# Immediates for the Ln, and features laid out in pairs of heads

## Chip, core and metric

The kernel runs on one core of a Trainium2 chip. Its time is the device time of one execution in microseconds, as a median over runs. The engines are named as in the profile: PE (TensorE, matmuls; PEld is its weight load), DVE (VectorE), ACT (ScalarE), POOL (GpSimd) and SP (SyncE, which issues most DMAs).

## The reference, cut to what matters

Two layers of linear attention with an exponential feature map, each followed by a gated MLP, over 2048 tokens of 512 elements, 32 heads of 16:

```python
def _A_ref(x, wqkv, w_phi, wo):
    ...
    pq = jnp.einsum("bhsd,hdf->bhsf", q, w_phi)
    pk = jnp.einsum("bhsd,hdf->bhsf", k, w_phi)
    phi_q = jnp.concatenate([_softmax(pq, axis=-1), _softmax(-pq, axis=-1)], axis=-1)
    phi_k = jnp.concatenate([_softmax(pk, axis=-1), _softmax(-pk, axis=-1)], axis=-1)
    kv = jnp.einsum("bhsf,bhsd->bhfd", phi_k, v)
    z  = jnp.einsum("bhsf->bhf", phi_k)
    num = jnp.einsum("bhqf,bhfd->bhqd", phi_q, kv)
    den = jnp.einsum("bhqf,bhf->bhq", phi_q, z)[..., None] + 1e-6
    o = num / den
    return (...o...) @ wo
...
x = x + _A_ref(_layernorm(x, axis=-1), A_wqkv, A_w_phi, A_wo)
x = x + _B_ref(_layernorm(x, axis=-1), B_W_gate, B_W_up, B_W_down)
x = x + _A_ref(_layernorm(x, axis=-1), A_wqkv, A_w_phi, A_wo)
x = x + _B_ref(_layernorm(x, axis=-1), B_W_gate, B_W_up, B_W_down)
```

A softmax over 16 features does not change when the last feature is subtracted from all, so the kernel folds that into the weights: 15 exponentials are computed, the 16th is 1, and the sum that scales them is 1 plus the sum of the 15.

## The kernel before, in words

The 2048 tokens are 16 tiles of 128 rows (partitions). The order of every instruction on every engine is written out in a list (ORDER), as are the buffers that each step takes (SLOTS) and, for steps that two engines can do, the engine (PLACE). Nothing is decided at run time: each engine works through its own list and waits on semaphores, and SP's DMAs are issued in the order of the list too.

For a tile of **keys** (class Keys): statistics of x on DVE (L510, L511), then the reciprocal standard deviation on ACT as exp(-0.5 ln(v + eps)) (L518 is the Ln with `bias=eps[:]`, L520 the Exp, rsA), the normalized tile xn on DVE or POOL (L534, L532), a transpose of it (PE L500 or SP L495), then the K matmul with folded weights (PE L596), the V matmul (PE L601) and its copy to SBUF (vext, L453 or L454). Two Exp of 480 elements on ACT (L568, one with scale 1 and one with -1) write the features into an `ek` tile; a reduction on DVE sums 64 groups of 15 (L606, sk); Ln with `bias=unit[:]` (L615, lnk) and Exp with scale -1 (L618, rk) on ACT make the 64 scales and put them into the same tile; a multiplication in two halves of 480 elements (L554, phi) on POOL or DVE scales the features; and the kvz matmuls (PE L629) add them up over all tiles.

An `ek` tile has 8 groups of 128 columns, a group for 4 heads. Before, a group is 60 positive features, 60 negative ones, and 8 scales at its end:

```python
e.tensor_tensor(out=v, in0=v, in1=ek.t[:, lo:lo + n, 2 * GF:P].unsqueeze(3).to_broadcast(
    [P, n, 2 * HG, DF]), op=Alu.mult)
```

so each scale is read 15 times at step 0, against 15 adjacent features.

For a tile of **queries**: the matmul (PE L656), the same two Exp, a reduction (L661, sq), Ln with the unit bias (L666) and Exp (L668) on half of the sums, the ratio on DVE (L672), one multiplication of 480 elements (L677, POOL or DVE), and a DMA transpose of the tile (SP L682, fq). Queries use tiles whose last constants were set to one at the start (ONES, on POOL).

When the keys of all tiles are done, R is built from their sums and a mask Mg on DVE (L641, L646); Mg is made at the start from the identity (L435, L437, L439). Then come, tile by tile, erq (PE L693), its division (L700 to L707), a transpose of o, the projection (PE L716), the residual sum (L720), and the MLP in blocks of 1 to 4 tiles (gate and up PE L793 and L769, down PE L833). The first layer's keys come first; the second layer's keys are worked in between the first layer's MLP blocks. The weights for queries are folded while the keys run: wq is loaded (SP, L866), transposed by DMA (SP L467) and multiplied (PE L481).

Of the kernel before, what the change touches and what calls it, by code (L numbers as in the profile page):

```python
# [8 lines left out]
P = 128  # L9
D = 512  # L10
H = 32
DH = 16
# [6 lines left out]
HB = 8  # L19
NG = 2 * NB  # L20
HG = HB // 2
# [3 lines left out]
DF = DH - 1  # L25
GF = HG * DF
FW = H * DF
EPS = 1e-5
DEN_EPS = 1e-6

Alu = mybir.AluOpType
AF = mybir.ActivationFunctionType
AX = mybir.AxisListType
BF16 = mybir.dt.bfloat16
F32 = mybir.dt.float32
# [89 lines left out]
DVE0 = (85, 170)  # L125
# [3 lines left out]
NOTHING = (0, 0)  # L129
# [151 lines left out]
def kernel(  # L281
    ctx: ExitStack, tc: tile.TileContext, A_x, A_wqkv, A_w_phi, A_wo, B_x, B_W_gate, B_W_up,
    B_W_down, out):
    nc = tc.nc
# [8 lines left out]
    def new(name, shape, dt=BF16):  # L293
        return sb.tile([P] + shape, dt, name=name)
# [14 lines left out]
    wf = new("wf", [NB, DH])  # L309
    wgu, wd = new("wgu", [2, NB, F]), new("wd", [NF, D])  # L310
    ident = new("ident", [P])
    Mf, Mg, Mh = new("Mf", [HB], F32), new("Mg", [HG], F32), new("Mh", [HG], F32)
    Wblk = new("Wblk", [NB, HB * DF])
    R = new("R", [NG, GE])
    xnTA = [new(f"xnTA{c}", [C, NB, P]) for c in range(C)]
    eps, unit = new("eps", [1], F32), new("unit", [1], F32)
    rowsum, ssq = new("rowsum", [2, T], F32), new("ssq", [2, T], F32)
    wasteA, wasteD = new("wasteA", [D]), new("wasteD", [D])
    st = {(l, s): (new(f"bst{s}{l}", [T, 6], F32), new(f"mv{s}{l}", [T, 2], F32),
# [25 lines left out]
    def op(eng, cost, due, emit, deps=(), takes=(), uses=(), name="", **kw):  # L345
        o = Op(eng, cost, due, emit, deps, takes, uses, name, **kw)
        ops.append(o)
        return o
# [52 lines left out]
    def first_constants():  # L401
        make_identity(nc, ident[:])
        for i in ONES:
            nc.gpsimd.memset(p_eq.tiles[i][:, :, 2 * GF + HG:P], 1.0)
    c_id = op("POOL", (900, 900), 0, first_constants, name="ident")
    def constants():
        nc.vector.memset(eps[:], EPS)
        nc.vector.memset(unit[:], 1.0)
    c_eps = op("DVE", DVE0, 0, constants, name="eps")
    ones = [op("DVE", DVE0, i, (lambda v: lambda: nc.vector.memset(v[:, :, GQ:GV], 1.0))(v), name="ones")  # L410
            for i, v in enumerate(p_v.tiles)]

    hr_zero = [op("DVE", dve(4 * (P - FR), 4), 9000, (lambda v: lambda: nc.vector.memset(v[:, :, FR:P], 0.0))(v),
                  name="hr0", port=True) for v in p_hr.tiles]
# [17 lines left out]
    c_blk = op("DVE", (640, 740), 20, lambda: blocks(nc.vector), [c_m, c_cen], name="Wblk", port=True,  # L432
               alt=("POOL", (1016, 1058), lambda: blocks(nc.gpsimd), 3))
    def state_masks():
        nc.vector.tensor_reduce(out=Mg[:], in_=ident[:, 0:2 * GF].rearrange("p (s h f) -> p h s f", s=2, f=DF),  # L435
                                axis=AX.XY, op=Alu.add)
        nc.vector.tensor_reduce(out=Mh[:], in_=ident[:, 2 * GF:P].rearrange("p (s h) -> p h s", s=2), axis=AX.X,  # L437
                                op=Alu.add)
        nc.vector.tensor_tensor(out=Mg[:], in0=Mg[:], in1=Mh[:], op=Alu.add)  # L439
    c_mg = op("DVE", (400, 490), 15000, state_masks, [c_m], name="Mg")  # L440
    wps = Buf(p_q)

    one = nc.const_aps.tensor(1.0, (P, 512), BF16)
# [69 lines left out]
    def norm_A(l, tiles, dues, afters, by_pe=False):  # L513

        _, mv, rs, ln = st[l, "A"]
        t0, n = tiles[0], len(tiles)
        seen = [stats(l, "A", t, due, after) for t, due, after in zip(tiles, dues, afters)]
        a = op("ACT", ACT1, dues[-1], lambda: nc.scalar.activation(  # L518
            out=ln[:, t0:t0 + n], in_=mv[:, t0:t0 + n, 1], func=AF.Ln, scale=1.0, bias=eps[:]), seen + [c_eps], name="ln")
        a = op("ACT", ACT0, dues[-1], lambda: nc.scalar.activation(  # L520
            out=rs[:, t0:t0 + n], in_=ln[:, t0:t0 + n], func=AF.Exp, scale=-0.5), [a], name="rstd")
        made, i = [], 0
        while i < n:
            k = 1 if by_pe or i + 1 == n else 2
            xn, scaled = Buf(p_xn), []
            for j in range(k):
                t = tiles[i + j]

                def on_pool(t=t, j=j, xn=xn):
                    nc.gpsimd.tensor_scalar(out=nm[:, t:t + 1], in0=mv[:, t, 0:1], scalar1=-1.0, scalar2=0.0,  # L530
                                            op0=Alu.mult, op1=Alu.add)
                    nc.gpsimd.tensor_scalar(out=xn.t[:, j], in0=x_of(t), scalar1=nm[:, t:t + 1],  # L532
                                            scalar2=rs[:, t:t + 1], op0=Alu.add, op1=Alu.mult)
                scaled.append(op("DVE", SCALE, dues[i + j], lambda t=t, j=j, xn=xn: nc.vector.tensor_scalar(  # L534
                    out=xn.t[:, j], in0=x_of(t), scalar1=mv[:, t, 0:1], scalar2=rs[:, t:t + 1],
                    op0=Alu.subtract, op1=Alu.mult), [a], [] if j else [xn], [xn] if j else [], name="xnA", port=2,
                    alt=("POOL", (930, 975), on_pool, 3) if l == 0 else None))
            c, r = tiles[i] // C, tiles[i] % C
            made += [turn(xn, lambda c=c, r=r, k=k: xnTA[c][:, r:r + k], k, dues[i], scaled, [], [], "xnTA",
                          by_pe)] * k  # L540
            i += k
        return made


    def features(ek, lo=0, n=NG):
        return ek.t[:, lo:lo + n, 0:2 * GF].rearrange("p g (j f) -> p g j f", f=DF)

    def halves(name, ek, engs, due, after, uses):
        parts = []
        n = NG // len(engs)  # L550

        def phi(e, lo):
            v = features(ek, lo, n)
            e.tensor_tensor(out=v, in0=v, in1=ek.t[:, lo:lo + n, 2 * GF:P].unsqueeze(3).to_broadcast(  # L554
                [P, n, 2 * HG, DF]), op=Alu.mult)
        for k, e in enumerate(engs):
            ways = {"DVE": ("DVE", dve(480), lambda k=k: phi(nc.vector, k * n), 1),
                    "POOL": ("POOL", (956, 998), lambda k=k: phi(nc.gpsimd, k * n), 3)}
            _, cost, f, _ = ways[e]
            parts.append(op(e, cost, due, f, after, [], uses, name=name,  # L560
                            port=ways[e][3], alt=ways["POOL" if e == "DVE" else "DVE"]))
        return parts

    def raised(ek, ps, s, side):
        assert side == "K" or ek.slot in ONES and ek.slot not in spoilt
        if side == "K":
            spoilt.add(ek.slot)
        nc.scalar.activation(out=ek.t[:, :, s * GF:(s + 1) * GF], in_=ps.t[:, 0:FW].rearrange(  # L568
            "p (g e) -> p g e", e=GF), func=AF.Exp, scale=1.0 - 2.0 * s)

    class Keys:
        def __init__(self, l, before):
# [8 lines left out]
        def begin(self, sk, row, t, due, due_v, due_z, xT, phi_eng, v_eng="ACT"):  # L581
# [13 lines left out]
            else:  # L595
# [8 lines left out]
            v = evac(v_eng, due_v, lambda: vx.t[:, :, 0:GQ], lambda: vp.t[:].rearrange("p (b e) -> p b e", e=GQ),  # L604
                     [v] + ones, [vx], [vp], "vext")
            a = op("DVE", SUM16, due, lambda: nc.vector.tensor_reduce(  # L606
                out=sk.t[:, row, :].rearrange("p (g j) -> p g j", g=NG), in_=features(ek), axis=AX.X, op=Alu.add),
                e, [] if row else [sk], [ek, sk] if row else [ek], name="sk")
            self.sk.append(a)
            self.ks.append(k)  # L610
# [2 lines left out]
        def finish(self, begun):  # L613
            (done, v, sk, ek, *rest), due = begun[0], begun[0][5]
            a = op("ACT", RLN[0], due, lambda: nc.scalar.activation(  # L615
                out=sk.t[:, 0, :], in_=sk.t[:, 0, :], func=AF.Ln, scale=1.0, bias=unit[:]), [done, c_eps], (), [sk],
                name="lnk")
            a = op("ACT", REXP[0], due, lambda: nc.scalar.activation(  # L618
                out=ek.t[:, :, 2 * GF:P], in_=sk.t[:, 0, :].rearrange("p (g j) -> p g j", g=NG), func=AF.Exp,
                scale=-1.0), [a], (), [sk, ek], name="rk")  # L620
            self.scale(a, v, ek, *rest)

# [30 lines left out]
    def query(l, t, due, xT, behind, key):  # L653
# [4 lines left out]
            for b in range(NB)], [xT] + q_fold, [qp, ek], name="Q", follow=key)  # L658
        e = [op("ACT", act(FW), due, lambda s=s: raised(ek, qp, s, "Q"), [q], (), [qp, ek], name="Eq")
             for s in range(2)]  # L660
        a = op("DVE", SUM16, due, lambda: nc.vector.tensor_reduce(  # L661
            out=sq.t[:].rearrange("p (g j) -> p g j", g=NG), in_=features(ek), axis=AX.X, op=Alu.add),
            e, [sq], [ek], name="sq", follow=behind)
        pos, neg = (lambda: sq.t[:].rearrange("p (g s h) -> p g s h", s=2, h=HG)[:, :, 0, :],
                    lambda: sq.t[:].rearrange("p (g s h) -> p g s h", s=2, h=HG)[:, :, 1, :])
        a = op("ACT", RLN[0], due, lambda: nc.scalar.activation(  # L666
            out=pos(), in_=pos(), func=AF.Ln, scale=1.0, bias=unit[:]), [a, c_eps], (), [sq], name="lnq")
        a = op("ACT", REXP[0], due, lambda: nc.scalar.activation(  # L668
            out=pos(), in_=pos(), func=AF.Exp, scale=-1.0), [a], (), [sq], name="rq")

        def ratio():
            nc.vector.scalar_tensor_tensor(out=ek.t[:, :, 2 * GF:2 * GF + HG], in0=neg(), scalar=1.0, in1=pos(), op0=Alu.add,  # L672
                                   op1=Alu.mult)

        def scale(e):
            v = ek.t[:, :, 0:GF].rearrange("p g (h f) -> p g h f", f=DF)
            e.tensor_tensor(out=v, in0=v, in1=ek.t[:, :, 2 * GF:2 * GF + HG].unsqueeze(3).to_broadcast(  # L677
                [P, NG, HG, DF]), op=Alu.mult)
        a = op("DVE", DVE0, due, ratio, [a], [], [ek, sq], name="rat", port=1, alt=("DVE", DVE0, ratio, 1))
        a = op("POOL", (956, 998), due, lambda: scale(nc.gpsimd), [a], [], [ek], name="phq", port=3,  # L680
               alt=("DVE", dve(480), lambda: scale(nc.vector), 1))
# [270 lines left out]
```

## Time and profile before

| | |
|---|---|
| median of 3 runs | 372.12 us (371.65 to 372.27) |
| profiled execution | 371.77 us |
| its span, first to last instruction | 370.0 us |
| PE busy | 361.4 us, 98% |
| DVE busy | 272.0 us, 74% |
| ACT busy | 203.4 us, 55% |
| POOL busy | 86.6 us, 23% |
| granted TensorE clock | 1.000 |

The span leaves out 1.77 us of the execution. Busy times are averages over stages that have different limits, so a row for one stretch of the span says more than the share of the whole. The ends of matmuls are modelled, so a busy PE need not be one at its peak. In a row of a group, the first two numbers behind the bar are its busy time in us and the mean duration of one in ns, and behind the second bar stands the idle time of the engine just before such instructions, with what ended it.

### The profile page before, as it was taken

The numbers are of one execution on the slowest core, as the hardware profiler recorded it, in microseconds if no ns is written. First come the engines' busy times: TensorE is split into PE (matmuls) and PEld (weight loads), VectorE is DVE, ScalarE is ACT, GpSimd is POOL, SyncE is SP. The second block draws the span as 40 slices with busy tenths as digits, with TensorE's granted clock in tenths as the row PEclk, the third lists the DMA queues.
The fourth block names the chain that finished last, engine by engine and source line by source line (L and its number), as shares of the span: only waits on it lengthen the run. The fifth ranks groups of instructions, "written<-read, shape, count | busy, mean of one in ns | idle before, by whom it ended". The sixth has DMA issues, their size and how long they took to land.

```text
span 370.0 us, 7444 instructions
## 1 busy us (share of the span) xinstructions
PE 361.4 (98%) x2803; PEld 217.0 (59%) x2845; DVE 272.0 (74%) x604; ACT 203.4 (55%) x549; POOL 86.6 (23%) x111
## 2 busy tenths in 40 slices
PE   8999999999999999999999999999999999999996
PEld 5454557776555454555666655686755454467484
DVE  6999999988798966848979498898976373233253
ACT  5999999662544860587274455874434226403130
POOL 4589754510030116004213173120000000000000
PEclk9999999999999999999999999999999999999999
DMA  8997776796653501113411210498752102010213
GB/s 239 195 225 161 235 123 128 128 151 126 96 101 58 99 16 30 37 22 64 85 36 31 57 32 0 69 134 121 137 99 45 28 0 44 0 44 0 81 54 98
DMA packets 93925, 31.73 MB, mean 86 GB/s; under 512 B 85345, under 2 KB 92865, under 8 KB 93889
## 3 DMA queue, kind: packets, MB, share of 16 engines
q1 hardware_dynamic: 93088, 30.98, 42.4%
q8 instruction: 22, 0.36, 0.4%
q10 hardware_dynamic: 800, 0.28, 0.3%
q14 instruction: 15, 0.11, 0.1%
HBM read 8.44 MB, written 2.10 MB: 28 GB/s over the span
## 4 chain that ended last, share of the span: by engine, by line
PE 84%; ACT 9%; DVE 2%; issue 1%; DMA 1%; POOL 1%; SPq 0%; DVEq 0%; ACTq 0%
PE b L793 38%; PE b L833 20%; PE b L716 7%; ACT ek L568 4%; PE b L601 4%; PE b L596 4%; PE b L656 4%; PE b L769 3%; PE q L693 2%; PE q L629 1%; ACT vext L453 1%; DMA X<-in_A_x_dram 1%; DVE sq L661 1%; ACT sk L615 1%; PE b L500 1%
## 5 line engine op out<-in xcount | busy, mean ns | idle before, releaser
L793 PE MATMUL b<-xnTB,wgu 128*128 128x128 bf16 (+2 forms) x1200 | 152.5, 279 | 0.1
L793 PEld LDWEIGHTS <-wgu 128*128 128x128 bf16 x1200 | 97.4, 98 | 47.2 <-issue 0.3
L797 ACT ACTIVATE gu<-b 128x512 bf16<-128x512 f32 (+1 forms) x83 | 47.6, 581 | 89.9 <-PE b L793 83.0
L833 PE MATMUL b<-wd,hT 128*128 128x512 bf16 (+3 forms) x340 | 83.2, 372 | 1.3
L568 ACT ACTIVATE ek<-b 128x480 bf16<-128x480 f32 x128 | 69.9, 597 | 16.1 <-PE b L596 8.6
L554 POOL TENSOR_TENSOR ek<-ek 128x480 bf16<-128x480 bf16 x48 | 49.5, 1055 | 79.2 <-ACT ek L618 74.6
L833 PEld LDWEIGHTS <-hT 128*128 128x128 bf16 (+1 forms) x363 | 34.3, 98 | 34.0 <-DVE hT L810 0.3
L810 DVE TENSOR_TENSOR hT<-gu,b 128x512 bf16<-128x512 bf16 (+1 forms) x44 | 28.6, 657 | 30.3 <-ACT gu L797 13.7
L677 POOL TENSOR_TENSOR ek<-ek 128x480 bf16<-128x480 bf16 x26 | 26.4, 1023 | 73.7 <-DVE ek L672 55.9
L661 DVE TENSOR_REDUCE sq<-ek 128x64 f32<-128x960 bf16 x32 | 36.4, 1144 | 4.1 <-ACT ek L568 4.1
L606 DVE TENSOR_REDUCE sk<-ek 128x64 f32<-128x960 bf16 x32 | 36.0, 1138 | 2.5 <-ACT ek L568 2.5
L801 DVE TENSOR_TENSOR hT<-gu 128x512 bf16<-128x512 bf16 (+1 forms) x39 | 17.2, 442 | 22.6 <-ACT gu L812 22.4
L840 DVE SCALAR_TENSOR_TENSOR X<-b,rsB,X 128x512 bf16<-128x512 f32 (+2 forms) x33 | 23.7, 729 | 12.9 <-PE b L833 12.7
L716 PE MATMUL b<-wo,oT 128*128 128x512 bf16 x117 | 30.8, 379 | 1.1 <-ACT oT L453 0.4
L601 PE MATMUL b<-wv,xnTA 128*128 128x512 bf16 x120 | 30.9, 379 | 0.6 <-ACT vext L453 0.2
L656 PE MATMUL b<-Wq,xnTA 128*128 128x480 bf16 x128 | 30.5, 365 | 0.1
L596 PE MATMUL b<-Wk,xnTA 128*128 128x480 bf16 x124 | 29.5, 366 | 0.0
L720 DVE SCALAR_TENSOR_TENSOR X<-b,X 128x512 bf16<-128x512 f32 x32 | 21.7, 684 | 6.0 <-PE b L716 5.8
L812 ACT CAST gu<-b 128x512 bf16<-128x512 f32 (+1 forms) x39 | 21.9, 573 | 6.8 <-PE b L793 6.6
L510 DVE BATCH_NORM_STATS2 bstA<-X 128x6 f32<-128x512 bf16 x32 | 21.4, 683 | 2.0 <-DMA X<-in_A_x_dram 1.7
L707 DVE TENSOR_TENSOR o<-q,rd 128x512 bf16<-128x512 f32 x32 | 21.9, 686 | 1.3 <-ACT rd L704 1.0
L601 PEld LDWEIGHTS <-xnTA 128*128 128x128 bf16 x128 | 12.0, 98 | 12.7 <-issue 0.3
(84 smaller groups left out, 346.4 us busy)
## 6 DMA issues: line engine op xcount, KB each, us to landing
out_dram<-X SPq DMA_DIRECT2D x15, 128.0 KB, 1.9
X<-in_A_x_dram SPq DMA_DIRECT2D x6, 256.0 KB, 4.8
wgu<-in_B_W_gate_dram SPq DMA_DIRECT2D x4, 344.0 KB, 3.7
wgu<-in_B_W_up_dram SPq DMA_DIRECT2D x4, 344.0 KB, 4.9
wd<-in_B_W_down_dram SPq DMA_DIRECT2D x5, 256.0 KB, 3.7
hT<-in_A_wqkv_dram SPq DMA_DIRECT2D x3, 256.0 KB, 4.4
X<-in_A_x_dram SPq DMA_DIRECT2D x4, 128.0 KB, 3.4
wv<-in_A_wqkv_dram SPq DMA_DIRECT2D x2, 256.0 KB, 4.8
```

Of the source, the lines that this page charges most:

```text
L554: e.tensor_tensor(out=v, in0=v, in1=ek.t[:, lo:lo + n, 2 * GF:P].unsqueeze(3).to_broadcast([P, n, 2 * HG, DF]), op=Alu.mult)
L568: nc.scalar.activation(out=ek.t[:, :, s * GF:(s + 1) * GF], in_=ps.t[:, 0:FW].rearrange("p (g e) -> p g e", e=GF), func=AF.Exp, scale=1.0 ...
L596: k = op("PE", mm(4, FW), due, lambda: [nc.tensor.matmul(kp.t[:, 0:FW], lhsT=xnTA[c][:, i, b, :], rhs=Wk2[:, b, :], start=(b == 0), stop=( ...
L601: v = op("PE", mm(4, 512), due_v, lambda: [nc.tensor.matmul(vp.t[:], lhsT=xnTA[c][:, i, b, :], rhs=wv[:, b, :], start=(b == 0), stop=(b == ...
L606: a = op("DVE", SUM16, due, lambda: nc.vector.tensor_reduce(out=sk.t[:, row, :].rearrange("p (g j) -> p g j", g=NG), in_=features(ek), axi ...
L656: q = op("PE", mm(4, FW), due, lambda: [nc.tensor.matmul(qp.t[:, 0:FW], lhsT=xnTA[c][:, i, b, :], rhs=Wq2[:, b, :], start=(b == 0), stop=( ...
L661: a = op("DVE", SUM16, due, lambda: nc.vector.tensor_reduce(out=sq.t[:].rearrange("p (g j) -> p g j", g=NG), in_=features(ek), axis=AX.X, ...
L716: a = op("PE", mm(4, 512), due + 3, lambda j=j, yp=yp: [nc.tensor.matmul(yp.t[:], lhsT=oT.t[:, j, b, :], rhs=wo[:, b, :], start=(b == 0), ...
L793: nc.tensor.matmul(ps.t[:, q * W:(q + 1) * W].rearrange("p (i t) -> p i t", t=P), lhsT=wgu[:, s, b, g * P:(g + 1) * P], rhs=xT.t[:, 0:n, b ...
L797: nc.scalar.activation(out=gu.t[:, 0, 0:cols], in_=gp.t[:, 0:cols], func=AF.Relu)
L810: nc.vector.tensor_tensor(out=h.t[:, f0 * W:f0 * W + cols], in0=gu.t[:, 0, 0:cols], in1=up.t[:, 0:cols], op=Alu.mult)
L833: nc.tensor.matmul(yp.t[:, 0:c1 - c0], lhsT=h.t[:m, f * W + i * P:f * W + (i + 1) * P], rhs=wd[:m, f, c0:c1], start=(f == 0), stop=(f == N ...
```

## The change

The bias of the three Ln becomes a number in the instruction; the tiles `eps` and `unit` and their two memsets go. A group of an `ek` tile is laid out as two pairs of heads; in each pair the positive and the negative features of two heads are interleaved (feature, then head of the pair), and the scale is the 16th feature of its head. A scaling therefore multiplies 15 rows of two adjacent features by one row of two adjacent scales, read 15 times. The two Exp write, and the reductions read, every second element. Mg becomes a single reduction over all columns, and Mh goes. The order of the instructions, the buffers and the engine of each step are the same lists as before.

```diff
-    Mf, Mg, Mh = new("Mf", [HB], F32), new("Mg", [HG], F32), new("Mh", [HG], F32)
+    Mf, Mg = new("Mf", [HB], F32), new("Mg", [HG], F32)
...
-    eps, unit = new("eps", [1], F32), new("unit", [1], F32)
...
-            nc.gpsimd.memset(p_eq.tiles[i][:, :, 2 * GF + HG:P], 1.0)
+            nc.gpsimd.memset(p_eq.tiles[i][:].rearrange("p g (k s f h) -> p s (g k) f h", k=2, s=2, h=2)[
+                :, 1, :, DF, :], 1.0)
...
-    def constants():
-        nc.vector.memset(eps[:], EPS)
-        nc.vector.memset(unit[:], 1.0)
-    c_eps = op("DVE", DVE0, 0, constants, name="eps")
+    c_eps = op("DVE", NOTHING, 0, lambda: None, name="eps")
...
-        nc.vector.tensor_reduce(out=Mg[:], in_=ident[:, 0:2 * GF].rearrange("p (s h f) -> p h s f", s=2, f=DF),
-                                axis=AX.XY, op=Alu.add)
-        nc.vector.tensor_reduce(out=Mh[:], in_=ident[:, 2 * GF:P].rearrange("p (s h) -> p h s", s=2), axis=AX.X,
-                                op=Alu.add)
-        nc.vector.tensor_tensor(out=Mg[:], in0=Mg[:], in1=Mh[:], op=Alu.add)
+        nc.vector.tensor_reduce(out=Mg[:].rearrange("p (k h) -> p k h", h=2), in_=ident[:].rearrange(
+            "p (k e h) -> p k h e", k=2, h=2), axis=AX.X, op=Alu.add)
...
-            out=ln[:, t0:t0 + n], in_=mv[:, t0:t0 + n, 1], func=AF.Ln, scale=1.0, bias=eps[:]), seen + [c_eps], name="ln")
+            out=ln[:, t0:t0 + n], in_=mv[:, t0:t0 + n, 1], func=AF.Ln, scale=1.0, bias=EPS), seen + [c_eps], name="ln")
...
-    def features(ek, lo=0, n=NG):
-        return ek.t[:, lo:lo + n, 0:2 * GF].rearrange("p g (j f) -> p g j f", f=DF)
+    def pairs(ek, s=None):
+        v = ek.t[:].rearrange("p g (k s f h) -> p (g k s) f h", k=2, s=2, h=2)
+        return v if s is None else v.rearrange("p (b s) f h -> p s b f h", s=2)[:, s]
+
+    def spread(ek, v, n):
+        return v[:, :, DF:DH, :].to_broadcast([P, n, DF, 2])
+
+    def summed(v):
+        return v[:, :, 0:DF, :].rearrange("p b f h -> p b h f")
...
-            v = features(ek, lo, n)
-            e.tensor_tensor(out=v, in0=v, in1=ek.t[:, lo:lo + n, 2 * GF:P].unsqueeze(3).to_broadcast(
-                [P, n, 2 * HG, DF]), op=Alu.mult)
+            v = pairs(ek)[:, lo:lo + n]
+            e.tensor_tensor(out=v[:, :, 0:DF, :], in0=v[:, :, 0:DF, :], in1=spread(ek, v, n), op=Alu.mult)
...
-        nc.scalar.activation(out=ek.t[:, :, s * GF:(s + 1) * GF], in_=ps.t[:, 0:FW].rearrange(
-            "p (g e) -> p g e", e=GF), func=AF.Exp, scale=1.0 - 2.0 * s)
+        nc.scalar.activation(out=summed(pairs(ek, s)), in_=ps.t[:, 0:FW].rearrange(
+            "p (b h f) -> p b h f", h=2, f=DF), func=AF.Exp, scale=1.0 - 2.0 * s)
...
-                out=sk.t[:, row, :].rearrange("p (g j) -> p g j", g=NG), in_=features(ek), axis=AX.X, op=Alu.add),
+                out=sk.t[:, row, :].rearrange("p (b h) -> p b h", h=2), in_=summed(pairs(ek)), axis=AX.X, op=Alu.add),
...
-                out=sk.t[:, 0, :], in_=sk.t[:, 0, :], func=AF.Ln, scale=1.0, bias=unit[:]), [done, c_eps], (), [sk],
+                out=sk.t[:, 0, :], in_=sk.t[:, 0, :], func=AF.Ln, scale=1.0, bias=1.0), [done, c_eps], (), [sk],
...
-                out=ek.t[:, :, 2 * GF:P], in_=sk.t[:, 0, :].rearrange("p (g j) -> p g j", g=NG), func=AF.Exp,
+                out=pairs(ek)[:, :, DF, :], in_=sk.t[:, 0, :].rearrange("p (b h) -> p b h", h=2), func=AF.Exp,
...
-            out=pos(), in_=pos(), func=AF.Ln, scale=1.0, bias=unit[:]), [a, c_eps], (), [sq], name="lnq")
+            out=pos(), in_=pos(), func=AF.Ln, scale=1.0, bias=1.0), [a, c_eps], (), [sq], name="lnq")
...
-            v = ek.t[:, :, 0:GF].rearrange("p g (h f) -> p g h f", f=DF)
-            e.tensor_tensor(out=v, in0=v, in1=ek.t[:, :, 2 * GF:2 * GF + HG].unsqueeze(3).to_broadcast(
-                [P, NG, HG, DF]), op=Alu.mult)
+            v = pairs(ek, 0)
+            e.tensor_tensor(out=v[:, :, 0:DF, :], in0=v[:, :, 0:DF, :], in1=spread(ek, v, DH), op=Alu.mult)
```

The sums, the ratio and the columns of ones of the queries follow the same layout.

More of the change, by code (lines that the diff above doesn't have):

```diff
@@ L434, in state_masks @@
     def state_masks():
-        nc.vector.tensor_reduce(out=Mg[:], in_=ident[:, 0:2 * GF].rearrange("p (s h f) -> p h s f", s=2, f=DF),
-                                axis=AX.XY, op=Alu.add)
-        nc.vector.tensor_reduce(out=Mh[:], in_=ident[:, 2 * GF:P].rearrange("p (s h) -> p h s", s=2), axis=AX.X,
-                                op=Alu.add)
-        nc.vector.tensor_tensor(out=Mg[:], in0=Mg[:], in1=Mh[:], op=Alu.add)
-    c_mg = op("DVE", (400, 490), 15000, state_masks, [c_m], name="Mg")
+        nc.vector.tensor_reduce(out=Mg[:].rearrange("p (k h) -> p k h", h=2), in_=ident[:].rearrange(
+            "p (k e h) -> p k h e", k=2, h=2), axis=AX.X, op=Alu.add)
+    c_mg = op("DVE", (230, 330), 15000, state_masks, [c_m], name="Mg")
     wps = Buf(p_q)
@@ L542, in norm_A @@
         return made
-    def features(ek, lo=0, n=NG):
-        return ek.t[:, lo:lo + n, 0:2 * GF].rearrange("p g (j f) -> p g j f", f=DF)
+    def pairs(ek, s=None):
[5 more added lines that the diff above has]
+        return v[:, :, 0:DF, :].rearrange("p b f h -> p b h f")
     def halves(name, ek, engs, due, after, uses):
         parts = []
-        n = NG // len(engs)
+        n = H // len(engs)
         def phi(e, lo):
-            v = features(ek, lo, n)
-            e.tensor_tensor(out=v, in0=v, in1=ek.t[:, lo:lo + n, 2 * GF:P].unsqueeze(3).to_broadcast(
-                [P, n, 2 * HG, DF]), op=Alu.mult)
+            v = pairs(ek)[:, lo:lo + n]
+            e.tensor_tensor(out=v[:, :, 0:DF, :], in0=v[:, :, 0:DF, :], in1=spread(ek, v, n), op=Alu.mult)
         for k, e in enumerate(engs):
@@ L661, in query @@
         a = op("DVE", SUM16, due, lambda: nc.vector.tensor_reduce(
-            out=sq.t[:].rearrange("p (g j) -> p g j", g=NG), in_=features(ek), axis=AX.X, op=Alu.add),
+            out=sq.t[:].rearrange("p (b h) -> p b h", h=2), in_=summed(pairs(ek)), axis=AX.X, op=Alu.add),
             e, [sq], [ek], name="sq", follow=behind)
-        pos, neg = (lambda: sq.t[:].rearrange("p (g s h) -> p g s h", s=2, h=HG)[:, :, 0, :],
-                    lambda: sq.t[:].rearrange("p (g s h) -> p g s h", s=2, h=HG)[:, :, 1, :])
+        pos, neg = (lambda: sq.t[:].rearrange("p (b s h) -> p s b h", s=2, h=2)[:, 0],
+                    lambda: sq.t[:].rearrange("p (b s h) -> p s b h", s=2, h=2)[:, 1])
         a = op("ACT", RLN[0], due, lambda: nc.scalar.activation(
-            out=pos(), in_=pos(), func=AF.Ln, scale=1.0, bias=unit[:]), [a, c_eps], (), [sq], name="lnq")
+            out=pos(), in_=pos(), func=AF.Ln, scale=1.0, bias=1.0), [a, c_eps], (), [sq], name="lnq")
         a = op("ACT", REXP[0], due, lambda: nc.scalar.activation(
@@ L671, in ratio @@
         def ratio():
-            nc.vector.scalar_tensor_tensor(out=ek.t[:, :, 2 * GF:2 * GF + HG], in0=neg(), scalar=1.0, in1=pos(), op0=Alu.add,
+            nc.vector.scalar_tensor_tensor(out=pairs(ek, 0)[:, :, DF, :], in0=neg(), scalar=1.0, in1=pos(), op0=Alu.add,
                                    op1=Alu.mult)
         def scale(e):
-            v = ek.t[:, :, 0:GF].rearrange("p g (h f) -> p g h f", f=DF)
-            e.tensor_tensor(out=v, in0=v, in1=ek.t[:, :, 2 * GF:2 * GF + HG].unsqueeze(3).to_broadcast(
-                [P, NG, HG, DF]), op=Alu.mult)
+            v = pairs(ek, 0)
+            e.tensor_tensor(out=v[:, :, 0:DF, :], in0=v[:, :, 0:DF, :], in1=spread(ek, v, DH), op=Alu.mult)
         a = op("DVE", DVE0, due, ratio, [a], [], [ek, sq], name="rat", port=1, alt=("DVE", DVE0, ratio, 1))
```

## The prediction

> **What bounds the kernel now.** I read the page first (parts 1 and 2), then the busy time of each engine by stretch, then the chain that ended last, and last the timeline around the few places where PE waits.
>
> ```profile
> span 370.0 us, 7444 instructions
> ...
> PE 361.4 (98%) x2803; PEld 217.0 (59%) x2845; DVE 272.0 (74%) x604; ACT 203.4 (55%) x549; POOL 86.6 (23%) x111
> ```
>
> ```profile
> 0.00:10.00 10.00, 8.87 (x71) 5.34 (x72) 6.77 (x26) 6.11 (x16) 4.86 (x25) 1.00 0.83 249
> 10.00:20.00 10.00, 9.95 (x62) 4.98 (x64) 9.94 (x24) 9.94 (x30) 6.33 (x12) 1.00 0.93 186
> 20.00:30.00 10.00, 9.49 (x80) 5.17 (x79) 9.77 (x17) 10.00 (x31) 8.74 (x12) 1.00 1.05 227
> 30.00:40.00 10.00, 9.91 (x67) 4.97 (x68) 10.00 (x12) 10.00 (x31) 9.04 (x9) 1.00 0.84 184
> 40.00:50.00 10.00, 9.74 (x88) 5.35 (x88) 9.88 (x14) 9.97 (x32) 6.07 (x7) 1.00 0.52 161
> 50.00:60.00 10.00, 8.95 (x95) 5.13 (x93) 9.73 (x19) 9.40 (x28) 6.29 (x6) 1.00 1.03 185
> 60.00:100.00 40.00, 39.49 (x420) 29.01 (x424) 35.83 (x93) 22.72 (x69) 7.98 (x9) 1.00 0.71 116
> 100.00:225.00 125.00, 124.37 (x775) 68.89 (x785) 95.91 (x196) 68.11 (x183) 31.57 (x31) 1.00 0.26 51
> ```
>
> The columns are PE, PEld, DVE, ACT, POOL, the granted clock, the DMA share and GB/s. The shares over the whole span hide two different stages. From 60 us on PE alone is full (39.49 of 40, 124.37 of 125), so a shorter instruction on ACT, DVE or POOL buys nothing there. From 10 to 50 us, the keys of the first layer, DVE and ACT are as full as PE (9.8 to 10.0 of 10), POOL nearly so from 20 to 40. The gain is therefore capped by PE's idle time ahead of 60 us: 1.13 us in the first stretch and 0.05 + 0.51 + 0.09 + 0.26 + 1.05 = 1.96 us in the next five. A busy matmul's end is modelled and runs past the start of the next, so a little more hides in each wait:
>
> ```profile
> L596 PE MATMUL b<-Wk,xnTA 128*128 128x480 bf16 x124 | 29.5, 366 | 0.0
> ```
>
> ```profile
> 17.70 0.24 ACT sk L615
> ...
> 18.89 0.16 ACT ek L618
> ...
> 21.56 0.38 issue
> 21.94 0.43 ACT sk L615
> 22.37 0.14 ACT ek L618
> 22.52 0.46 ACT ek L568
> ...
> 26.55 0.81 PE b L596 x4
> ...
> 34.70 0.21 ACT sq L666
> ...
> 41.13 0.13 ACT sq L668
> ```
>
> A 480-column matmul counts 0.366 us busy, but in the chain four of them pass in 0.81, so 0.16 us of each wait is covered. These rows are pieces of the chain between 17 and 42 us: it runs through ACT, whose instructions follow one another without waits, with PE at times (26.55).
>
> **The change part by part.** *Immediates.* The Ln instructions lose a per-partition bias operand:
>
> ```profile
> L615 ACT ACTIVATE sk<-sk,unit 128x64 f32<-128x64 f32 x32 | 11.9, 382 | 5.8 <-DVE sk L606 5.8
> ...
> L666 ACT ACTIVATE sq<-sq,unit 128x32 f32<-128x32 f32 x32 | 10.6, 336 | 2.8 <-DVE sq L661 2.5
> ...
> L668 ACT ACTIVATE sq<-sq 128x32 f32<-128x32 f32 x32 | 7.6, 236 | 0.4
> ```
>
> L666 and L668 have the same shape and type and differ by the operand: 336 against 236 ns. In the chain, where only the distance to the next instruction counts, it is 0.21 against 0.13, and 0.24 against 0.14 to 0.16 for L615 and L618. I take 0.09 us each. Half of the 32 L615 (the first layer's), the first layer's ten L518 (four single tiles, six pairs) and about three L666 run ahead of 50 us: 29 x 0.09 = 2.6 us off ACT where ACT is full. The other 55 lie under a full PE and are worth nothing.
>
> *The scaling on DVE.* The scale operand was one element read 15 times; it becomes a row of two adjacent ones read 15 times, all bf16.
>
> ```profile
> L554 POOL TENSOR_TENSOR ek<-ek x48: 985/994/1465, 17.8 to 227.6; 128x480 bf16<-128x480 bf16 x48
> ...
> L554 DVE TENSOR_TENSOR ek<-ek x16: 642/654/1404, 31.7 to 227.5; 128x480 bf16<-128x480 bf16 x16
> ```
>
> ```profile
> L677 POOL TENSOR_TENSOR ek<-ek x26: 996/1002/1421, 44.9 to 245.2; 128x480 bf16<-128x480 bf16 x26
> ...
> L677 DVE TENSOR_TENSOR ek<-ek x6: 642/649/658, 46.4 to 259.4; 128x480 bf16<-128x480 bf16 x6
> ```
>
> ```profile
> L801 DVE TENSOR_TENSOR hT<-gu x39: 286/420/1212, 71.5 to 359.5; 128x512 bf16<-128x512 bf16 x37, 128x256 bf16<-128x256 bf16 x2
> ```
>
> ```profile
> 25.00:50.00 25.00, 4.38 (x6) 16.88 (x17) 1.00 0.73 190
> 50.00:62.00 12.00, 0.95 (x2) 2.31 (x2) 1.00 0.86 154
> ```
>
> (The last fence is line L554 alone: DVE, then POOL.) No row has the new pattern. The bounds are 654 ns (no change) and L801, dense bf16 with both inputs in SBUF: 286 ns at 256 and 420 at 512 elements, 0.52 ns an element, so 403 at 480. I take 403, as the new operands are rows of adjacent elements throughout, and keep 654 for a rival. Six L554 and one L677 before 50 us and two L554 just after then shed 9 x 0.25 = 2.25 us of DVE. [...]
>
> *The scaling on POOL.* Same 480 elements; the scale operand goes from 32 rows of 15 to 240 rows of 2, and L554's other operands from 4 rows to 16.
>
> ```profile
> L426 POOL TENSOR_TENSOR Wblk<-wf,Mf 128x480 bf16<-128x480 bf16 x1 | 1.0, 1000 | 1.0 <-DVE mvA L511 1.0
> ```
>
> L426 re-reads its first operand in 32 rows and takes 1000 ns, 6 above L554's 994 with 4 rows: 0.2 ns a row. L677 has 8 rows in operand and result and takes 1002: at worst 2 ns a row. For 208 more rows that is 0.04 to 0.42 us. I take 0.04, since L426 has by far the most rows; that little lies in POOL's free time. A faster POOL would help only in the two L554 at 50.44 below.
>
> *Exp and sum.* L568 now writes every second bf16 (a step of 4 bytes) and L606/L661 read so. DVE's reduction has a row with a wider step:
>
> ```profile
> L606 DVE TENSOR_REDUCE sk<-ek 128x64 f32<-128x960 bf16 x32 | 36.0, 1138 | 2.5 <-ACT ek L568 2.5
> ...
> L435 DVE TENSOR_REDUCE Mg<-ident 128x4 f32<-128x120 bf16 x1 | 0.3, 268 | 0.0
> ...
> L437 DVE TENSOR_REDUCE Mh<-ident 128x4 f32<-128x8 bf16 x1 | 0.1, 150 | 0.0
> ```
>
> L437 reads 8 elements four apart. From it to L435 the slope is 118/112 = 1.05 ns an element, from L435 to L606 870/840 = 1.04: the step costs nothing. For ACT's write there is no row; I take nothing and price it as a rival.
>
> *Start of DVE.* L437, the add behind it and two memsets go, and L435 reads 8 columns more (0.01 us); DVE then still waits for x, so nothing comes of it:
>
> ```profile
> 3.34 0.69 DVE L510 BATCH_NORM_STATS2 bstA<-X 128x6 f32<-128x512 bf16 x1 [1.08 <-DMA X<-in_A_x_dram]
> ```
>
> No wait is added, and the order on every engine and queue stays.
>
> **The sum**, where PE waits:
>
> ```profile
> 9.97 0.39 PE L592 MATMUL b<-Wblk,gu 128*128 128x120 bf16 x4 [0.16 <-ACT gu L453]
> ```
>
> ```profile
> 21.03 1.23 SPq L467 DMA_TRANSPOSE hT<-hT  x1
> ...
> 24.83 0.43 PEld L481 LDWEIGHTS <-hT 128*128 128x128 bf16 x8 [0.87 <-DMA hT<-hT]
> ```
>
> ```profile
> 50.44 2.31 POOL L554 TENSOR_TENSOR ek<-ek 128x480 bf16<-128x480 bf16 x2 [2.31 <-DVE ek L554]
> ...
> 52.81 0.30 PE L629 MATMUL q<-vext,ek 128*128 128x65 bf16 x4 [0.41 <-POOL ek L554]
> ```
>
> - To 25 us: three L518 stand ahead of the copy that PE awaits at 9.97, 0.27 us. But at 24.83 PE waits for the transpose of wq issued at 21.03, whose load is behind the xn transposes on SP, and these follow rsA. DVE sheds nothing here, and every sk that ACT awaits is DVE's (the 0.38 at 21.56). I take 0.3 us (0 to 0.45).
> - 25 to 50 us: ACT sheds 16 x 0.09 = 1.4 and DVE 7 x 0.25 = 1.75 us, more than PE can use: its idle time is 0.09 + 0.26 plus some four covered 0.16, 0.9 at most. I take half, 0.45.
> - The last keys: POOL's two L554 come behind ACT and DVE, both earlier by more than PE's wait, 0.41 + 0.16. I take 0.55.
> - From there R, erq, o and their transposes follow that last kvz at unchanged lengths: nothing.
>
> Sum 1.3 us. The profiled execution took 371.77 us, 1.77 around its span; 370.5 after. The median of the runs is 0.35 above it, 372.12, so I forecast **370.8**. With PE's whole idle time from 10 to 60 us gone (1.96 and seven covered 0.16, 3.1 us) it would be 369.0; with PE using half of what I took, 371.5.
>
> **The rivals.** (a) *DVE stays the bound*: rows of two are not paired, L554 stays at 654. For: DVE is full from 10 us, and the sk that ACT awaits come from it, so ACT's 2.6 us turn into waits for DVE. Against: the chain is on ACT. What is left is the 0.3 us to 25 us and some 0.1 behind it: gain 0.4, **371.7**.
>
> (b) *POOL becomes the bound, slower*: rows of two cost it 2 ns each, L554 takes 1.41 us. POOL is busy 8.74 + 9.04 of 20 us from 20 to 40 us with 16 L554; 16 x 0.42 = 6.7 us do not fit into 2.2 free ones, PE's kvz waits 4.5 us more, **375.3**. It decides from 2.2/16 = 0.14 us more an instruction. Against: L426. [...]
>
> (c) *ACT's strided write is slower*: its 48 L568 ahead of 50 us are 0.46 apart in the chain. At 0.1 us more each, 4.8 against 2.6 saved, and none of the gain: 372.1 + 2.2 = **374.3**; it decides from 2.6/48 = 0.05 us. No row speaks for it.
>
> **How the numbers follow.** Forecast 0.62, (a) 0.19, (b) 0.11, (c) 0.08. About 0.2% (0.74 us) is what a measurement of this kernel can tell from no change; (a) falls inside, (b) and (c) slower: faster 0.62, same 0.19, slower 0.19. The range reaches from the low bound of the sum, 369.0, through (a) and what lies 0.2% above, and a mild (c), to 373.2; it leaves out (b) and most of (c).
>
> **What would show it.** Right: L615, L666 and L518 down by 0.09 to 0.10 us, L554 and L677 near 0.40 on DVE and 1.0 on POOL, L568 and L606 unchanged, and PE's wait at the last kvz gone with 60 us work starting 1.3 us earlier. Wrong: POOL above 1.13 us, L568 spaced over 0.5, or DVE at 0.65 with new ACT waits for sk.

## The result

The changed kernel takes **376.11 us** (median of 4 runs, 375.96 to 376.49) against 372.12 before: a ratio of 1.0111, 95% interval 1.0093 to 1.0128. The forecast was 370.8 us with a range up to 373.2. The kernel became slower, for the larger part by the mechanism of rival (c), ACT's write with a step. The kernel before was run again beside the experiments: its median is 371.87 us beside the first three full kernels below and 371.70 beside the last four, and each ratio there is taken against these runs.

The page after the change: the span, busy time by engine, the shares of the chain that ended last, and the costliest group on ACT (behind the first bar its busy us and mean ns of one).

```profile
span 374.2 us, 7440 instructions
...
PE 362.2 (97%) x2803; PEld 216.7 (58%) x2845; DVE 267.0 (71%) x600; ACT 210.5 (56%) x549; POOL 84.5 (23%) x111
...
PE 81%; ACT 13%; DVE 2%; issue 2%; DMA 1%; POOL 1%; SPq 0%; DVEq 0%; ACTq 0%; POOLq 0%
...
L568 ACT ACTIVATE ek<-b 128x480 bf16<-128x480 f32 x128 | 88.9, 807 | 15.3 <-PE b L596 7.7
```

DVE has 5.0 us less to do than before (272.0), as intended. ACT has 7.1 us more (203.4 before), although its Ln are shorter. The Exp of L568 by itself, durations as minimum, median and maximum in ns, in the kernel before:

```profile
L568 ACT ACTIVATE ek<-b x128: 550/580/740, 12.1 to 243.8; 128x480 bf16<-128x480 f32 x128
```

and in the kernel after:

```profile
L568 ACT ACTIVATE ek<-b x128: 712/756/1169, 11.6 to 247.1; 128x480 bf16<-128x480 f32 x128
```

All 128 are longer, by 0.18 us in the median, and the shortest after (712) is longer than the median before (580), so it isn't a few of them that met a wait. Not all of a duration is paid in the chain: before, 0.58 in the median stands against 0.46 from one Exp to the next. What the path pays is read from the chain of waits, here before:

```profile
19.14 1.84 ACT ek L568 x4
20.98 0.23 ACT sk L615
```

and after:

```profile
19.03 2.35 ACT ek L568 x4
21.38 0.09 ACT sk L615
...
22.90 0.63 ACT ek L568
```

Four Exp in a row go from 1.84 to 2.35 us, 0.13 each; the single one goes from the 0.46 of the prediction's row at 22.52 to 0.63, 0.17: the sign of error that the prediction named, L568 spaced over 0.5. The Ln between them fell from 0.23 to 0.09, and to 0.14 or 0.15 elsewhere in that chain. The windows of after (columns as in the prediction) show what that does to the stage:

```profile
20.00:30.00 10.00, 9.19 (x76) 4.94 (x74) 9.57 (x17) 10.00 (x30) 8.09 (x10) 1.00 0.91 219
30.00:40.00 10.00, 9.16 (x63) 4.56 (x63) 8.96 (x12) 10.00 (x27) 7.25 (x9) 1.00 0.74 147
40.00:50.00 10.00, 9.69 (x70) 4.84 (x70) 7.28 (x12) 9.97 (x33) 7.63 (x8) 1.00 0.45 163
```

DVE came free (8.96 and 7.28 where it was full), PE fell from 9.91 to 9.16 between 30 and 40 us, and ACT alone is full from 20 to 50. The gain on DVE was real and had nobody to go to.

The last piece of the chain tells how much of the loss arose on PE. Before:

```profile
362.95 3.50 PE b L833 x21
```

After:

```profile
366.06 3.50 PE b L832 x21
```

PE ends 3.11 us later, but the span is 4.2 us longer. The remaining 1.1 us lie behind PE, at the last store. The DMA view of the end of the run, first before (from 365 us), then after (from 368 us); the last number of the store's row is the time from issue to landing:

```profile
out_dram<-X SPq DMA_DIRECT2D x1, 32.0 KB, 1.5
```

```profile
out_dram<-X SPq DMA_DIRECT2D x1, 32.0 KB, 2.6
```

In a window that begins at 371.85 us, when most of that store has been moved, the trace of after has this left:

```profile
DMA packets 10, 0.01 MB, mean 4 GB/s; under 512 B 9, under 2 KB 9, under 8 KB 9
## 3 DMA queue, kind: packets, MB, share of 16 engines
q14 instruction: 1, 0.01, 0.8%
q1 hardware_dynamic: 9, 0.00, 0.5%
```

One packet of 8 KB of the queue that the trace calls instruction (q14), and nine small packets of the store, which come behind it (from 372.27 us, when it ended). In the trace of before no such packet lies behind 353.5 us. So two questions go to the experiments: is it the step of the write, and what is the packet doing there?

### The profile page after: what moved, and what is told of

Its sections match the earlier page's. It is cut to its first block, busy times and chain, and to the rows that moved or that the text cites. A ratio compares the mean times of both kernels' runs of the same rounds, so it can differ in the third digit from the quotient of the medians.

```text
span 374.2 us, 7440 instructions
## 1 busy us (share of the span) xinstructions
PE 362.2 (97%) x2803; PEld 216.7 (58%) x2845; DVE 267.0 (71%) x600; ACT 210.5 (56%) x549; POOL 84.5 (23%) x111
## 4 chain that ended last, share of the span: by engine, by line
PE 81%; ACT 13%; DVE 2%; issue 2%; DMA 1%; POOL 1%; SPq 0%; DVEq 0%; ACTq 0%; POOLq 0%
PE b L792 37%; PE b L832 20%; ACT ek L568 8%; PE b L715 7%; PE b L656 4%; PE b L596 4%; PE b L601 3%; PE b L768 3%; PE q L692 2%; ACT vext L447 1%; PE q L629 1%; DMA X<-in_A_x_dram 1%; PE b L494 1%; ACT ek L618 1%; POOL ek L555 1%
## 5 line engine op out<-in xcount | busy, mean ns | idle before, releaser
L792 PE MATMUL b<-xnTB,wgu 128*128 128x128 bf16 (+2 forms) x1200 | 152.5, 279 | 0.1
L792 PEld LDWEIGHTS <-wgu 128*128 128x128 bf16 x1200 | 97.4, 98 | 47.1 <-issue 0.5
L796 ACT ACTIVATE gu<-b 128x512 bf16<-128x512 f32 (+1 forms) x83 | 47.9, 585 | 89.0 <-PE b L792 82.5
L568 ACT ACTIVATE ek<-b 128x480 bf16<-128x480 f32 x128 | 88.9, 807 | 15.3 <-PE b L596 7.7
L555 POOL TENSOR_TENSOR ek<-ek 128x480 bf16<-128x480 bf16 x48 | 48.2, 1026 | 82.2 <-ACT ek L618 76.8
L677 POOL TENSOR_TENSOR ek<-ek 128x480 bf16<-128x480 bf16 x26 | 25.7, 997 | 76.5 <-DVE ek L672 58.4
L606 DVE TENSOR_REDUCE sk<-ek 128x64 f32<-128x960 bf16 x32 | 36.1, 1141 | 5.1 <-ACT ek L568 4.3
```

What stands on the lines that cost most here:

```text
L555: e.tensor_tensor(out=v[:, :, 0:DF, :], in0=v[:, :, 0:DF, :], in1=spread(ek, v, n), op=Alu.mult)
L568: nc.scalar.activation(out=summed(pairs(ek, s)), in_=ps.t[:, 0:FW].rearrange("p (b h f) -> p b h f", h=2, f=DF), func=AF.Exp, scale=1.0 - ...
L606: a = op("DVE", SUM16, due, lambda: nc.vector.tensor_reduce(out=sk.t[:, row, :].rearrange("p (b h) -> p b h", h=2), in_=summed(pairs(ek)), ...
L792: nc.tensor.matmul(ps.t[:, q * W:(q + 1) * W].rearrange("p (i t) -> p i t", t=P), lhsT=wgu[:, s, b, g * P:(g + 1) * P], rhs=xT.t[:, 0:n, b ...
L796: nc.scalar.activation(out=gu.t[:, 0, 0:cols], in_=gp.t[:, 0:cols], func=AF.Relu)
```

## The experiments

**The Exp alone.** A kernel of ACT instructions only: the same 480 elements from PSUM, eight times for each way of writing. It leaves out the whole computation of the reference. Most of the ways (two further ones with adjacent elements, 16 rows of 30 and 120 rows of 4, took 569 and 570 ns); yA is the layout before in rows and yB the layout after:

```python
yD: out=yD[:, 0:480]                                                  # 480 adjacent
yA: out=... "p (r c) -> p r c", c=128, [:, :, 0:60]                   # 8 rows of 60
yB: out=... "p (b s f h) -> p s b h f", s=2, f=16, h=2, [.., 0:15]    # 16 x 2 rows of 15 at step 2
yF: out=... "p (b f) -> p b f", f=16, [:, :, 0:15]                    # 32 rows of 15 at step 1
yH: out=... "p (b f) -> p b f", f=4, [:, :, 0:2]                      # 240 rows of 2
yE: out=... "p (f h) -> p h f", h=2, [:, 0]                           # 480 at step 2
yG: out=... "p (b f h) -> p h b f", f=16, h=2, [:, 0, :, 0:15]        # 32 rows of 15 at step 2
yM: out=yM[:, 0:480] "p (f h) -> p h f", h=2                          # 2 x 240 at step 2, together 480 adjacent
yI: out=... 16 rows of 30, in_=... "p (b h f) -> p b f h"             # written in order, read at step 15
yJ: as yB into float32
yK: as yD into float32
```

> Exp alone, 480 elements from PSUM, eight back to back for each destination pattern; the rest of the kernel is left out. In the changed kernel the distance from one Exp to the next is 0.63 us, before 0.46. Theory 1 (the step): a destination step of 4 bytes costs ACT per element, whatever the rows: 16x2x15 at step 2, 480 at step 2, 32x15 at step 2 and 2x240 at step 2 all lie near 0.63; 8x60, 16x30, 32x15 at step 1 and 240x2 at step 1 near 0.46. Theory 2 (the rows): each new destination row costs some 7 ns (0.17 us for 24 more rows): 32x15 is near 0.63 at either step, 480 at step 2 stays at 0.46, 16x30 is near 0.52 and 240x2 over 2 us. Theory 3 (contention): the instruction itself is not slower, DVE and POOL disturb it in the kernel: all patterns near 0.46. With fp32 output the step is 8 bytes: by theory 1 at least as slow as bf16.

Groups by line in that kernel:

```profile
L48 ACT ACTIVATE yG<-ps 128x480 bf16<-128x480 f32 x8 | 5.9, 737 | 0.2
L33 ACT ACTIVATE yB<-ps 128x480 bf16<-128x480 f32 x8 | 5.8, 724 | 0.2
L42 ACT ACTIVATE yE<-ps 128x480 bf16<-128x480 f32 x8 | 5.6, 702 | 0.2
L66 ACT ACTIVATE yM<-ps 128x480 bf16<-128x480 f32 x8 | 5.6, 701 | 0.2
L57 ACT ACTIVATE yJ<-ps 128x480 f32<-128x480 f32 x8 | 4.8, 601 | 0.2
L30 ACT ACTIVATE yA<-ps 128x480 bf16<-128x480 f32 x8 | 4.6, 571 | 0.2
L45 ACT ACTIVATE yF<-ps 128x480 bf16<-128x480 f32 x8 | 4.6, 572 | 0.2
L39 ACT ACTIVATE yD<-ps 128x480 bf16<-128x480 f32 x8 | 4.6, 570 | 0.2
L54 ACT ACTIVATE yI<-ps 128x480 bf16<-128x480 f32 x8 | 4.6, 570 | 0.2
...
L60 ACT ACTIVATE yK<-ps 128x480 f32<-128x480 f32 x8 | 4.6, 570 | 0.2
...
L51 ACT ACTIVATE yH<-ps 128x480 bf16<-128x480 f32 x8 | 4.6, 569 | 0.2
```

At step 1 the number of rows costs nothing: 240 rows of two take as long as 480 elements in one (569 and 570). The step costs 132 ns with nothing else changed (yE), 153 in the layout of the change (yB against yA), and 167 in 32 rows (yG), so rows add up to 35 ns once there is a step. What counts is the order within the instruction: two bf16 written one after the other side by side cost nothing (yH, 569), but two halves at step 2 that leave 480 adjacent elements behind cost as much as yE (yM, 701). Reading PSUM at a step of 15 costs nothing here (yI, 570). So the theory of the step stands against that of the rows, with one part of it refuted: float32 was expected to be at least as slow, and the same step in elements costs it 31 ns (yJ against yK). The distance from one Exp to the next, busy and idle time of the eight taken together, is 0.60 us for yA (4.6 and 0.2) and 0.75 for yB (5.8 and 0.2), above the 0.46 and 0.63 that were expected; what carries over is the difference. Contention with other engines explains at most a small part of it: of the 176 ns between the medians in the full kernels 153 are here too, where no other engine computes beside ACT from 7 us on.

**The two parts of the change apart.** The kernel before with only the three biases as numbers and the two tiles gone:

```diff
-            out=ln[:, t0:t0 + n], in_=mv[:, t0:t0 + n, 1], func=AF.Ln, scale=1.0, bias=eps[:]), ...
+            out=ln[:, t0:t0 + n], in_=mv[:, t0:t0 + n, 1], func=AF.Ln, scale=1.0, bias=EPS), ...
```

> The kernel before with the biases as immediates and nothing else. Main theory (ACT is the bound of the first layer's keys, so what it sheds or gains there moves the end): 29 Ln ahead of 50 us shed 0.09 us each; PE has little idle time to give back, so 0.5 to 1.2 us less than before, 371.2. Rival (DVE's reductions are as much the bound and take up ACT's savings): within 0.3 us of before, 372.0.

Measured: 370.41 us (370.1 to 371.05), ratio 0.9965, interval 0.9952 to 0.9979. That is 1.46 less than the runs beside it, where 0.5 to 1.2 was expected, and it reaches the forecast for the whole change with this part alone. And the layout alone, the kernel after with `eps[:]` and `unit[:]` put back:

> The changed kernel with the biases as per-partition operands again. Main theory: ACT, now the only bound of the keys, gets 29 x 0.09 = 2.6 us more, nearly all of which shows: 378.0 (377.5 to 378.7). Rival (the time lost lies elsewhere than on ACT): no more than 0.5 above the changed kernel, 376.5.

Measured: 378.43 us (378.11 to 378.56), ratio 1.0177, interval 1.0163 to 1.0191, as expected. The layout is what loses.

**The write repaired, twice.** First by the order of the columns of the folded weights (feature, then head), so that PSUM holds the pairs already and both sides of the Exp run in order; the block matrix is made by two instructions on POOL instead of one:

```diff
-            "p (b h f) -> p b h f", h=2, f=DF), func=AF.Exp, scale=1.0 - 2.0 * s)
+            "p (b f h) -> p b f h", h=2, f=DF), func=AF.Exp, scale=1.0 - 2.0 * s)
...
+        for h in range(2):
+            e.tensor_tensor(out=Wblk[:].rearrange("p b (k f h) -> p b k f h", f=DF, h=2)[:, :, :, :, h], ...
```

> The changed kernel, but the columns of the folded weights are laid out as feature, then head of the pair, so that the matmul delivers the interleaved order and each Exp writes 16 rows of 30 adjacent elements; the immediates, the scalings and the sums are as in the changed kernel, and the mask for the weights is made by two POOL instructions in place of one. Theory 1 (step): Exp back at 0.46 us, and the forecast's sum comes true: 370.8 (369.5 to 371.6). Theory 2 (rows): Exp near 0.52, 48 x 0.06 = 2.9 us more on ACT against 2.6 saved: 372.1. If ACT's Exp is not the cause: 376.

Measured: 370.82 us (370.43 to 370.88), ratio 0.9969, interval 0.9958 to 0.9981. That it is the number of the forecast is in part luck, since this kernel has the late store too (below). Then by one line of the kernel after, which visits the same elements in another order:

```diff
-        nc.scalar.activation(out=summed(pairs(ek, s)), in_=ps.t[:, 0:FW].rearrange(
-            "p (b h f) -> p b h f", h=2, f=DF), func=AF.Exp, scale=1.0 - 2.0 * s)
+        nc.scalar.activation(out=pairs(ek, s)[:, :, 0:DF, :], in_=ps.t[:, 0:FW].rearrange(
+            "p (b h f) -> p b f h", h=2, f=DF), func=AF.Exp, scale=1.0 - 2.0 * s)
```

> The kernel after with one line changed: the Exp goes through its 480 elements in the order in which they lie in the ek tile (16 rows of 30 adjacent bf16), and so reads PSUM at a step of 15 elements, instead of reading PSUM in order and writing every second bf16. The same bytes are written to the same places. Theory (the step of the write costs ACT about 0.17 us an Exp): the Exp falls from 0.76 to 0.58 us, and the time from 376.1 to about 370.8, as with the permuted weights; the last store still lands late, since DVE has as many instructions as in the kernel after. Rival (any step on either side of ACT costs, the read as much as the write): the Exp stays above 0.70 us and the time above 374.

Measured: 371.02 us (370.52 to 371.55), ratio 0.9975, interval 0.9965 to 0.9985. L568 in this kernel:

```profile
L568 ACT ACTIVATE ek<-b x128: 549/574/695, 11.7 to 241.7; 128x480 bf16<-128x480 f32 x128
```

Every byte goes where it went in the kernel after; only the order within the instruction differs, and 5.1 us come back (376.11 to 371.02). That settles the cause of the larger part of the loss.

**The last store.** The kernel after and both repaired ones have 600 DVE instructions on the page of their profile, the kernel before 604, and the immediates alone and the layout alone 602. In the repaired ones the last store is late as well (landing 2.5 and 2.4 us after its issue, with an 8 KB packet of queue 14). The place of the last such packet goes with that number: it begins 16.5 us ahead of the end of the span in the kernel before, 3.7 and 3.8 in the two with 602, and 2.3 to 2.4 in the three with 600, and only in these is the store late. Four small memsets at the start of DVE restore the count:

```diff
-    c_eps = op("DVE", NOTHING, 0, lambda: None, name="eps")
+    spare = new("spare", [1], F32)
+    def fill():
+        for _ in range(4):
+            nc.vector.memset(spare[:], 1.0)
+    c_eps = op("DVE", NOTHING, 0, fill, name="eps")
```

In the kernel after:

> The kernel after with four small memsets on DVE at the start, so that DVE has as many instructions as in the kernel before. Theory: of the 4 us that the kernel after lost, 1.1 are an 8 KB fetch of instructions (queue 14 in the trace) that stands in front of packets of the last store, because the removed DVE instructions moved it there; with the count restored it falls elsewhere, the last store lands 1.5 us after its issue instead of 2.6, and the time is 375.0. Rival (the late last store has another cause, such as the stores before it): 376.1, and the last store still lands after 2.6.

Measured: 375.2 us (374.97 to 375.39), ratio 1.0089, interval 1.0075 to 1.0103. That interval overlaps with the one without the memsets (1.0093 to 1.0128), so the times alone don't decide; the traces do. The last 56 gate and up matmuls (L792 there, L796 here) begin no earlier than in the kernel after, at 362.98 against 362.82, and yet the span is 373.3 against 374.2: the store lands 1.5 us after its issue. And together with the one line of the read order:

> Both edits together: the Exp writes in the tile's order and DVE has its four memsets. Theory: the two causes add, 376.1 - 5.3 - 1.1 = 369.7, below the immediates alone (370.4) by what the faster scaling on DVE brings. Rival (the late store is nothing of the fetch's): 370.8.

Measured: **369.74 us** (369.6 to 370.01), ratio 0.9944, interval 0.9931 to 0.9956, the fastest of all. The DMA view of the last microseconds of this kernel (queues, then the last store):

```profile
q1 hardware_dynamic: 288, 0.13, 17.7%
...
out_dram<-X SPq DMA_DIRECT2D x1, 32.0 KB, 1.5
```

No packet of queue 14 is left there and the store lands after 1.5 us, in this kernel and in the one before it; no such packet lies in the last 7.3 us of either. The intervals with and without the memsets (0.9931 to 0.9956 against 0.9965 to 0.9985) don't meet. Four instructions more on DVE made this kernel 1.3 us faster (371.02 to 369.74).

**The scaling on DVE alone.** The permuted weights with the tile biases put back, so that of the gains of the change only the shorter scaling is left:

> The layout in pairs with permuted weights, so that the Exp writes rows of 30 adjacent bf16, and the Ln with their tile biases as in the kernel before: the faster scaling on DVE alone. DVE has as many instructions as in the kernel with the immediates alone, whose last store was not late. Theory (ACT sets the pace up to 50 us, so that a shorter instruction on DVE is worth little without the immediates): 371.2, 0.7 under the kernel before. Rival (ACT and DVE are alternatives that draw on the same idle time of PE, and each brings nearly all of it alone): 370.3.

Measured: 371.37 us (371.14 to 372.54), ratio 0.9994, interval 0.9985 to 1.0002. That is 0.3 less than its runs of before, where 0.7 was expected, and not to be told from nothing: while ACT sets the pace, a shorter instruction on DVE is worth little. That the two edits are alternatives, each of which brings nearly all of the gain alone, is refuted for this one.

## Why the prediction was wrong, point by point

- **Immediates: right.** In the kernel that has only them, the Ln cost what the Exp of the same shape beside them cost (L662 is the prediction's L666, L664 its L668):

```profile
L664 ACT ACTIVATE sq<-sq 128x32 f32<-128x32 f32 x32 | 7.5, 236 | 0.4
L662 ACT ACTIVATE sq<-sq 128x32 f32<-128x32 f32 x32 | 7.5, 239 | 2.7 <-DVE sq L657 2.6
```

  336 to 239, 0.10 us as stated. 2.6 us off ACT was the term where ACT is full. Between the layout alone (6.6 over its runs of before) and the filled kernel after (3.5 over), where ACT sets the pace for most of the first layer's keys, the immediates are worth 3.1 us; with the old layout, where PE takes over, 1.5.

- **The scaling on DVE: right in size.** In the kernel after:

```profile
L555 DVE TENSOR_TENSOR ek<-ek x16: 392/408/957, 32.0 to 230.4; 128x480 bf16<-128x480 bf16 x16
```

  654 to 408 ns, where 403 was taken. The 403 was an estimate from L801's two lengths, and it held; what in the engine makes the rows of two so much shorter is not shown.

- **The scaling on POOL: right.** 988 ns against 994; the 1.41 us of rival (b) never came:

```profile
L555 POOL TENSOR_TENSOR ek<-ek x48: 982/988/1436, 17.8 to 230.5; 128x480 bf16<-128x480 bf16 x48
```

- **Exp and sum: here the prediction failed.** Its half on the reduction held (L606 at 1141 ns against 1138, though it now reads at a step). The other half was "For ACT's write there is no row; I take nothing". The row that was near, L437, is a read on another engine and bounds nothing of a write on ACT. No upper end was taken into the sum, and the rival with it got a chance of 0.08 and a price of 0.1 us, with "No row speaks for it" as the reason, as if a missing row were one against it. The price was 0.13 to 0.17 in the chain. 48 Exp at 0.13 are 6.2 us; less the 2.6 of the immediates 3.6. The filled kernel after lost 3.5. That the rival's way of adding comes out so well with the right term is in part luck, since it has the whole loss arise with the first layer's keys. The chain of the kernel after shows less of it there and the rest later (its last kvz matmuls, a group of the first MLP blocks, and a piece of the second layer):

```profile
55.01 0.32 PE q L629 x4
...
70.95 1.79 PE b L792 x32
...
227.25 1.32 ACT ek L568 x2
```

  The first group began at 52.81 before and the second (there L793) at 68.29: 2.2 us are lost by the end of the first layer's keys, 2.7 by 71 us, 3.1 at PE's end. Behind 60 us, where the prediction has PE alone full, the slower Exp comes back into the chain.

- **Start of DVE: wrong by a way that wasn't looked at.** "Nothing comes of it" held for the start. But with fewer instructions (600 against 604) an 8 KB packet of the instruction queue came in among the packets of the last store, which landed 2.6 us after its issue instead of 1.5, and cost about 1 us at the end.

- **The sum.** With the write repaired alone, 371.02 stands beside the 370.8 forecast, but that closeness is luck: the late store costs 1.3, and the gain without it is larger than 1.3 us. With both repaired it is 2.0 us (371.70 to 369.74). The windows of that kernel:

```profile
20.00:30.00 10.00, 10.00 (x85) 5.62 (x84) 9.94 (x17) 10.00 (x33) 8.88 (x12) 1.00 0.95 230
30.00:40.00 10.00, 9.99 (x70) 4.99 (x68) 10.00 (x13) 10.00 (x30) 8.95 (x10) 1.00 0.84 188
40.00:50.00 10.00, 10.00 (x90) 5.50 (x89) 9.73 (x17) 9.92 (x32) 6.06 (x7) 1.00 0.68 170
```

  PE is full from 20 to 50 us, where the prediction took half of its idle time. Part of this is the trace and not the kernel: it has records of 2845 matmuls, as many as weight loads, the one of the kernel before 2803, and from 100 to 225 us PE reads 125.00 here and 124.37 there. The last keys came as forecast: PE no longer waits for POOL, and the block of matmuls runs through (timeline of the same kernel; its last four stood alone at 52.81 before, behind a wait of 0.41):

```profile
49.31 1.94 POOL L559 TENSOR_TENSOR ek<-ek 128x480 bf16<-128x480 bf16 x2 [2.48 <-ACT ek L622]
...
51.08 0.67 PE L633 MATMUL q<-vext,ek 128*128 128x65 bf16 x16
```

  R, which follows them, begins 1.4 us earlier than before, so up to there the 1.3 of the sum came. (In the repaired kernel without the memsets it is 1.8, so 0.4 us of such a comparison come from something else than the layout.) The rest came later, where the prediction has "nothing", as one and the same group of matmuls near the end shows, before and in this kernel:

```profile
359.71 3.13 PE b L793 x56
```

```profile
357.94 3.13 PE b L796 x56
```

  It is 1.8 us earlier. Which wait gave these 0.4 us after 53 us was not looked at by an experiment.

- **Rival (a)** had the right mechanism for another kernel: with the immediates alone, the Exp falls from 39.8 to 9.2% of the chain of waits from 10 to 50 us, PE takes most of it, and DVE's reduction stands in it with 12.8%. With the scaling shorter as well, the chain in that stretch is nearly all PE (96.4% in four of its lines). That the layout's own gain on top of the immediates is 0.7 us (369.74 against 370.41) is likely but not firmly shown: the intervals, 0.9931 to 0.9956 and 0.9952 to 0.9979, overlap a little.

## What to carry to other kernels

When a layout is changed for the engine that reads it, price the engine that writes it too, and where the trace has no row for that write, measure it or carry a real upper end in the sum: absence of a row is no evidence for zero. A repair can lie in the order in which one instruction visits its elements: put the step on the side that doesn't charge for it, here the read of PSUM (570 ns at a step of 15 elements, 570 in order), and let ACT write two adjacent bf16 one after the other (569 ns, against 701 to 737 at a step of two). When a small change moves the end of a kernel, look at what PE's end and the span each say, and at the last store.

## What the hardware showed unexpectedly

A bf16 write of ACT at a step of two elements took 132 to 167 ns more for 480 elements (702, 724 and 737 against 570 to 572), while rows of two adjacent elements (569), short rows (572) and a read of PSUM at a step of 15 elements (570) cost nothing, and float32 at the same step 31 ns.

A packet of the instruction queue stood in the way of data: in the kernel after, the one of 8 KB was under way from 371.95 for 0.32 us. All but nine of the store's packets had ended by 371.81. These nine began only as that packet ended, one behind the other, and the last ended at 372.43; eight of them carry 256 bytes each, together a sixteenth of the 32 KB, the share of one of the core's 16 DMA engines if each moves as much. The store landed at 373.29, 2.6 us after its issue instead of 1.5. The trace doesn't name the DMA engine of a packet; that they share one is read from these times. That the packet is for DVE was not read from the trace; it is inferred from the count of DVE instructions moving it, in both pairs of kernels in which only that count was changed (the store lands after 2.6 us with 600 and 1.5 with 604, and after 2.4 and 1.5).
